# One weight row moved to GpSimd's queue, and sixteen matmuls moved ahead of a projection, in a fused state-space and feed-forward block

## The chip, the core and the metric

The kernel runs on one core of a Trainium2 chip. The metric is the device time of one execution in microseconds (us). A core has five instruction streams that run side by side and wait for each other through semaphores: TensorE (PE, with its weight loads shown apart as PEld), VectorE (DVE), ScalarE (ACT), GpSimd (POOL) and SyncE (SP), which here only issues DMAs. SP, ACT and POOL issue DMAs; sixteen DMA engines carry them out.

## The reference

The input x has 2048 tokens of 512 numbers. The result is the sum of x and two branches, both fed by the layer norm of x:

```
xn  = layernorm(x)                              # mean and variance over the 512 features
A   = 2 Re(C h) + xn * Dskip,  h_t = Lam_bar h_(t-1) + B_bar xn_t     # complex, 512 states
B   = (silu(xn w_gate) * (xn w_up)) w_down      # 512 -> 1376 -> 512
out = x + A + B
```

Lam_bar and B_bar come from the parameter vectors Lambda_re, Lambda_im and log_dt. All tensors are bf16.

## The kernel before

**Tiling.** Tokens go in 16 tiles of 128 and in four chunks (0 to 3) of four tiles. Matmuls contract over 128 rows and give 128x512 results in PSUM, which has eight banks of that size; `bank()` hands them out in turn. The 1376 hidden features are ten full blocks of 128 and a rest of 96 (`FR`). `xnT` holds the normalized tokens transposed, which is what the matmuls need.

**Stages on PE.** (1) Warm-up matmuls (line 703). (2) The head: chunk 0 has no transposed tokens yet, so tiles 0 and 1 are transposed by matmuls against an identity (`raw_mm`, line 237), the mean is taken off by matmuls (`cT_mean`, line 245), and ACT and DVE copy the results out (`raw_copy`, line 252). Then `row_mm(which, k)` (line 747) multiplies both tiles with row k of the up weights (which = 0) or of the gate weights (which = 1): four matmuls of 128x512 for each k, four rows each, all at line 506. A row here is 128 of the 512 input features by the first 1024 hidden ones, 256 KB. (3) A transposition of the parameter vectors (`prm_transpose`, line 278), tile 2's transposition, and the other products of chunk 0 (lines 506 and 805). (4) Chunk 0's projection on the 512 states (`bproj_tile`, line 387, 32 matmuls with the transposed B matrix `BT`). (5) `gateup_last(0)` (line 548; matmuls at line 555): the last 96 features of chunk 0, 16 matmuls of 128x192, four evacuations on ACT (lines 560 and 561), and a product on DVE with a transposing DMA behind it (line 571). (6) The same for the other chunks: projections, gate and up (line 462), output matmuls with `w_down` (lines 620 and 630) and with C (line 643).

**Order.** Each engine's order is that of the program text (`manual_schedule`). DVE's long operations (tables, scans, rotations) stand in a backlog; `pump(us)` takes operations from it as PE time passes, `need(tag)` drains it up to a tag, and `multiply(keep)` runs waiting products from the list `products`.

**Loads at the start.** SP issues, in this order: tile 0 of x (line 128), the four up rows (lines 132 and 122), gate rows 0 and 1, tile 2 of x, gate row 2, tile 3, gate row 3, the last feature group of both weights (`load_w1`, line 118, tile `w_end`), and x of chunk 1 (line 146). ACT issues tile 1 of x (line 130). POOL builds the identity (`make_identity`, called at line 126), clears `prm_rows` (line 143), loads the three parameter vectors into it (line 145, three DMAs of 1 KB) and then computes the powers for the layer norm (line 199). The semaphores of SP's and ACT's DMAs are used in turn by eights: an issue waits until the DMA eight places before it has landed.

**Further DMAs.** Line 258 transposes chunk 0 into `xnT` in two parts, line 150 loads `BT` in two transposing DMAs (real and imaginary part), line 262 transposes chunks 1 to 3. At line 896, SP copies x of chunks 0 to 2 to the output in eight pieces of 192 rows, onto which POOL later adds results (lines 604 and 653).

Of the kernel before, what the change touches and what calls it, by code (L numbers as in the profile page):

```python
# [23 lines left out]
def kernel(  # L24
# [17 lines left out]
    nc = tc.nc  # L42
# [4 lines left out]
    CW = 512  # L47
    HW = CW // 2
    NT = L // 128
    NCH = L // CW  # L50
    TPC = CW // 128
    KD = D // 128
# [25 lines left out]
    def bank(shape=(128, CW), dtype=F32):  # L78
        return psum.tile(list(shape), dtype, name="ps")

    def flat(ap3):
        return ap3.rearrange("p q j -> p (q j)")
# [4 lines left out]
    wu_v = B_w_up.rearrange("(k p) f -> p k f", p=128)  # L87
# [8 lines left out]
    wu01 = const.tile([128, KD, FE], BF16, name="wu01")  # L96
# [24 lines left out]
    def load_row(q, t, view, k):  # L121
        q.dma_start(out=t[:, k, :], in_=view[:, k, 0:FE])  # L122

    HK = KD // 2
    ident = const.tile([128, 128], BF16, name="ident")
    make_identity(nc, ident[:])
    minus_mean = const.tile([128, 128], BF16, name="minus_mean")
    nc.sync.dma_start(out=xall[:, 0, :], in_=x_v[:, 0, :])  # L128
    nc.vector.memset(xall[:, 1, 0:2], 0.0)
    nc.scalar.dma_start(out=xall[:, 1, :], in_=x_v[:, 1, :])  # L130
    nc.scalar.preload_act_table_set("silu_and_others")
    for k in range(KD):
        load_row(nc.sync, wu01, wu_v, k)
    for k in range(HK):
        load_row(nc.sync, wg01, wg_v, k)
# [69 lines left out]
    def norm_dve(n):  # L205
        c, i = divmod(n, TPC)
        nc.vector.tensor_scalar(out=xn_tile(c)[:, :, i, :], in0=by_k(xall[:, n, :]), scalar1=mv[:, n, 0:1],
                                scalar2=rstd[:, n:n + 1], op0=ALU.subtract, op1=ALU.mult)
# [9 lines left out]
    SW = TPC - 1  # L218
# [57 lines left out]
    def prm_transpose():  # L276
        pp = bank()[:, 0:128]
        nc.tensor.matmul(pp, lhsT=prm_rows[:], rhs=ident[:], start=True, stop=True)  # L278
        return pp
# [4 lines left out]
    def exp_pool(out, in_):  # L284
        nc.gpsimd.tensor_tensor(out=out, in0=e_t[:], in1=in_, op=ALU.pow)
# [96 lines left out]
    def bproj_tile(c, part, q):  # L382
        if c not in u_tiles:
            u_tiles[c] = ssm.tile([128, 2, NQ, CW], BF16, name="u16", bufs=2)
        ps = bank()
        for k in range(KD):
            nc.tensor.matmul(ps[:] if c else by_k(ps[:]), lhsT=BT[:, part, k, q * 128:(q + 1) * 128],  # L387
                             rhs=xnT[:, c, k, :] if c else xnT0[:, k], start=(k == 0), stop=(k == KD - 1))
        nc.scalar.copy(out=u_tiles[c][:, part, q, :], in_=ps[:])  # L389
# [67 lines left out]
    products = []  # L457
# [10 lines left out]
    def gu_tile(c):  # L468
        if c not in gu_tiles:
            gu_tiles[c] = gut.tile([128, FT, CW], BF16, name="guT")  # L470
        return gu_tiles[c]
# [8 lines left out]
    def gu_rest(c):  # L480
        return gu_more_rest[:] if c == 2 else gu_tile(c)[:, FT - 1, 0:RT * 128]
# [21 lines left out]
    def sw_mm(ps, groups, gi, i, k0=0, k1=KD):  # L503
        a, b = fgroups[gi]
        for k in range(k0, k1):
            nc.tensor.matmul(ps[:, 0:(b - a) * 128], lhsT=tokens(i, k), rhs=groups[gi][:, k, 0:(b - a) * 128],  # L506
                             start=(k == 0), stop=(k == KD - 1))
# [35 lines left out]
    def g0_dma(a, b):  # L543
        nc.sync.dma_start_transpose(out=runs(gu_tiles[0][:, a:b, :]), in_=g0[:, a:b].rearrange("p f i d -> p (f i d)"))
# [3 lines left out]
    def gateup_last(c):  # L548
        gl = g_last[c % 2][:] if c else g0[:, FT - 1, 0:RT]
        u = up_p.tile([128, RT, 128], BF16, name="ul", bufs=2)  # L550
        for h in range(0, TPC, 2):
            ps = bank()[:, 0:4 * FR].rearrange("p (i w f) -> p i w f", i=2, w=2)
            for i in range(2):
                for k in range(KD):
                    nc.tensor.matmul(ps[:, i],  # L555
                                     lhsT=xnT[:, c, k, (h + i) * 128:(h + i + 1) * 128] if c else xnT0[:, k, h + i, :],
                                     rhs=w_end[:, k, :, FL - FE:FL - FE + FR], start=(k == 0), stop=(k == KD - 1))
            two = slice(h * RB, (h + 2) * RB)
            src = ps.rearrange("p i w (j f) -> p w j i f", f=RB)
            nc.scalar.activation(out=gl[:, :, two].rearrange("p j (i f) -> p j i f", f=RB), in_=src[:, 0], func=ACT.Silu)  # L560
            nc.scalar.copy(out=u[:, :, two].rearrange("p j (i f) -> p j i f", f=RB), in_=src[:, 1])

        def product():
            V.tensor_tensor(out=gl, in0=gl, in1=u[:], op=ALU.mult)
            if c:
                nc.sync.dma_start_transpose(out=gu_rest(c).rearrange("p (n t) -> p n t", t=128),
                                            in_=gl.rearrange("p i d -> p (i d)"))
            else:
                a = fgroups[1][1]
                n = (FT - 1 - a) * TPC + RT  # L570
                nc.sync.dma_start_transpose(
                    out=flat(gu_tile(0)[:, a:FT, :])[:, 0:n * 128].rearrange("p (n t) -> p n t", t=128),
                    in_=g0[:, a:FT].rearrange("p f i d -> p (f i d)")[:, 0:n * 128])
        products.append(product)
# [93 lines left out]
    def step():  # L668
        for item in backlog[0:AHEAD + 1]:
            if item[2] is not None:  # L670
                item[2]()
                item[2] = None
        cost, op, _, _ = backlog.pop(0)
        op()
        owed[0] -= cost

    def pump(us):

        owed[0] += us
        while backlog and owed[0] >= backlog[0][0] * 0.5:  # L680
            step()
        if not backlog:
            owed[0] = 0.0

    def multiply(keep):

        while len(products) > keep:
            products.pop(0)()
            owed[0] -= 0.65

    def need(tag):

        while any(item[3] == tag for item in backlog):
            step()


    GU = 8 * 0.2163
# [49 lines left out]
    def row_mm(which, k):  # L747
        for i in range(2):
            for gi in range(2):
                sw_mm(pair[which][i][gi], (U, G)[which], gi, i, k, k + 1)  # L750
# [8 lines left out]
            sw_up(gi, i, pair[0][i][gi])  # L759
    for n in range(2):  # L760
        norm_dve(n)
    row_mm(1, 0)
    pp = prm_transpose()
    ln_stats(2)
    center(2)
# [2 lines left out]
    ln_rstd(3, 4)  # L768
    prm_copy(pp)
    exp_pool(dt_t[:], ldt)  # L770
    for k in range(1, SW):
        row_mm(1, k)
    t2 = bank()
    for k in range(KD):
# [46 lines left out]
    def bproj_chunk(c):  # L821
        need(f"ln{c}")
        for part in range(2):
            for q in range(NQ):
                bproj_tile(c, part, q)
                pump(BP)
                multiply(0 if q else 1)
# [32 lines left out]
    def queue_ssm(c):  # L860
        fwd, back = ssm_ops(c)
        queue(f"ssm{c}", fwd + back)

    need("ln0")
    for part in range(2):
        for q in range(NQ):
            bproj_tile(0, part, q)
            pump(BP)
            multiply(0 if q else 1)
# [5 lines left out]
    queue("cf", c_ops())  # L875
    need("ln1")
    g0_dma(0, fgroups[1][1])
    gateup_last(0)
    pump(GU / 2)
    bproj_chunk(1)  # L880
    load_down()
    for part, src in enumerate((A_C_re, A_C_im)):
# [8 lines left out]
    gateup_chunk(1)  # L891
    nc.gpsimd.dma_start(out=dsk_bc[:], in_=A_Dskip.partition_broadcast(128))
    bproj_chunk(2)
    piece = (NCH - 1) * CW // 8
    for a in range(0, (NCH - 1) * CW, piece):
        nc.sync.dma_start(out=out[0, a:a + piece, :], in_=A_x[0, a:a + piece, :])
    queue_ssm(2)
    gateup_chunk(2)
    out_chunk(0)
# [45 lines left out]
```

## Time and profile before

| | us |
|---|---|
| median of three runs | 177.66 (177.65 to 178.03) |
| the profiled execution, whole | 178.12 |
| its span in the trace | 176.0 |
| PE busy | 171.0 |
| DVE busy | 157.4 |
| ACT busy | 102.3 |
| POOL busy | 27.1 |

The span runs from the first to the last instruction of the trace; 2.12 us of the execution lie around it. In the rows of the trace the first number is the start in us from the span's start, the second the duration in us (for merged rows, of the whole group); what follows is engine, line, operation, result, operands and count. "SPq" and "ACTq" are issues of DMAs from SP's and ACT's queues. "Busy" of a matmul counts from its start to its modelled end, and neighbouring matmuls overlap: four of them in a row start 0.22 us apart.

### The profile page before, as it was taken

The numbers are of one execution on the slowest core, as the hardware profiler recorded it, in microseconds if no ns is written. First come the engines' busy times: TensorE is split into PE (matmuls) and PEld (weight loads), VectorE is DVE, ScalarE is ACT, GpSimd is POOL, SyncE is SP. The second block draws the span as 40 slices with busy tenths as digits, with TensorE's granted clock in tenths as the row PEclk, the third lists the DMA queues.
The fourth block names the chain that finished last, engine by engine and source line by source line (L and its number), as shares of the span: only waits on it lengthen the run. The fifth ranks groups of instructions, "written<-read, shape, count | busy, mean of one in ns | idle before, by whom it ended". The sixth has DMA issues, their size and how long they took to land.

```text
span 176.0 us, 2435 instructions
## 1 busy us (share of the span) xinstructions
PE 171.0 (97%) x878; PEld 82.0 (47%) x894; DVE 157.4 (89%) x260; ACT 102.3 (58%) x188; POOL 27.1 (15%) x36
## 2 busy tenths in 40 slices
PE   8899999999999999999999999999999999999993
PEld 5444445564444464444444444446444444444542
DVE  3767999999999999999999999999999999589642
ACT  3179589794996689976044362014666652983100
POOL 5234110022000000000302500014100000530700
PEclk9999999999999999999999999999999999999999
DMA  5998969999999300220005830006310000597741
GB/s 152 370 342 80 194 110 181 303 202 293 169 207 274 115 4 0 50 61 0 2 4 111 94 34 0 0 4 68 53 22 0 0 4 0 70 164 124 93 89 60
DMA packets 34027, 18.05 MB, mean 103 GB/s; under 512 B 24512, under 2 KB 32832, under 8 KB 33888
## 3 DMA queue, kind: packets, MB, share of 16 engines
q1 hardware_dynamic: 30272, 14.39, 35.0%
q0 software_dynamic: 3456, 3.28, 14.6%
q10 hardware_dynamic: 288, 0.23, 0.4%
q8 instruction: 7, 0.11, 0.3%
q14 instruction: 4, 0.03, 0.1%
HBM read 8.33 MB, written 5.24 MB: 77 GB/s over the span
## 4 chain that ended last, share of the span: by engine, by line
PE 94%; DMA 3%; issue 1%; SPq 0%; ACT 0%; DVE 0%; ACTq 0%
PE ps L462 29%; PE ps L630 20%; PE ps L643 16%; PE ps L387 16%; PE ps L506 7%; PE ps L555 3%; DMA wu<-in_B_w_up_dram 3%; PE ps L805 2%; PE ps L620 2%; ACT u L489 0%; SPq L122 0%; SPq L128 0%; DVE xall L646 0%; PE ps L237 0%; PE ps L278 0%
## 5 line engine op out<-in xcount | busy, mean ns | idle before, releaser
L429 DVE TENSOR_TENSOR_SCAN g<-r_t,car,u 128x512 bf16<-128x512 f32 x24 | 28.8, 1263 | 0.0
L643 PE MATMUL ps<-CF,wt 128*128 128x512 bf16 (+2 forms) x133 | 28.2, 366 | 0.2
L387 PE MATMUL ps<-xnT,BT 128*128 128x512 bf16 x125 | 28.1, 379 | 0.2
L630 PE MATMUL ps<-wd_sb,guT 128*128 128x512 bf16 (+2 forms) x129 | 26.5, 362 | 0.1
L462 PE MATMUL ps<-xnT,wu 128*128 128x512 bf16 x94 | 24.5, 379 | 0.2
L462 PE MATMUL ps<-xnT,wg 128*128 128x512 bf16 x93 | 24.3, 379 | 0.1
L389 ACT CAST u<-ps 128x512 bf16<-128x512 f32 x32 | 17.8, 591 | 5.0 <-PE ps L387 4.1
L489 ACT CAST u<-ps 128x512 bf16<-128x512 f32 x30 | 17.8, 592 | 4.8 <-PE ps L462 4.8
L643 PEld LDWEIGHTS <-wt 128*128 128x128 bf16 x136 | 12.9, 98 | 15.0 <-DVE xall L600 0.4
L387 PEld LDWEIGHTS <-BT 128*128 128x128 bf16 x128 | 12.5, 98 | 14.9 <-DMA BT<-in_A_B_re_dram 0.3
L630 PEld LDWEIGHTS <-guT 128*128 128x128 bf16 x130 | 12.4, 98 | 13.8
L199 POOL TENSOR_TENSOR rstd<-ve,neg_half 128x1 f32<-128x1 f32 (+1 forms) x7 | 7.0, 1001 | 73.0 <-DVE ve L198 72.6
L652 ACT CAST res<-ps 128x512 bf16<-128x512 f32 x12 | 6.9, 582 | 18.5 <-PE ps L643 18.5
L592 ACT ACTIVATE xr<-xall,nb,rstd 128x512 bf16<-128x512 bf16 x16 | 11.8, 804 | 8.7 <-DVE xall L600 5.0
L653 POOL DMA_DIRECT2D out_dram<-res x12 | 10.5, 1043 | 35.6 <-ACT res L652 30.0
L462 PEld LDWEIGHTS <-wu 128*128 128x128 bf16 x96 | 9.4, 98 | 11.3
L488 ACT ACTIVATE guT<-ps 128x512 bf16<-128x512 f32 x20 | 12.1, 604 | 4.0 <-PE ps L462 3.6
L462 PEld LDWEIGHTS <-wg 128*128 128x128 bf16 x96 | 9.3, 98 | 10.6
L212 ACT ACTIVATE xn<-xall,nb,rstd 128x512 bf16<-128x512 bf16 x8 | 6.3, 816 | 8.8 <-DVE nb L202 8.8
L189 DVE BATCH_NORM_STATS2 stats<-xall 128x6 f32<-128x512 bf16 x16 | 10.8, 675 | 0.6 <-DMA xall<-in_A_x_dram 0.6
L462 PE MATMUL ps<-xnT,w_end 128*128 128x512 bf16 x47 | 10.8, 379 | 0.1
L397 DVE TENSOR_TENSOR pm<-g,c 128x2048 bf16<-128x2048 bf16 x8 | 9.8, 1222 | 0.1
(132 smaller groups left out, 235.3 us busy)
## 6 DMA issues: line engine op xcount, KB each, us to landing
out_dram<-in_A_x_dram SPq DMA_DIRECT2D x8, 192.0 KB, 3.2
out_dram<-res POOLq DMA_DIRECT2D x12, 128.0 KB, 3.1
out_dram<-xall POOLq DMA_DIRECT2D x3, 512.0 KB, 6.4
wd_sb<-in_B_w_down_dram SPq DMA_DIRECT2D x1, 1280.0 KB, 7.8
wu<-in_B_w_up_dram SPq DMA_DIRECT2D x4, 256.0 KB, 4.9
wg<-in_B_w_gate_dram SPq DMA_DIRECT2D x4, 256.0 KB, 5.5
xall<-in_A_x_dram SPq DMA_DIRECT2D x1, 1024.0 KB, 7.0
xall<-in_A_x_dram SPq DMA_DIRECT2D x1, 512.0 KB, 6.1
```

Of the source, the lines that this page charges most:

```text
L189: nc.vector.bn_stats(out=stats[:, n, 0, :], in_=xall[:, n, :])
L387: nc.tensor.matmul(ps[:] if c else by_k(ps[:]), lhsT=BT[:, part, k, q * 128:(q + 1) * 128], rhs=xnT[:, c, k, :] if c else xnT0[:, k], star ...
L389: nc.scalar.copy(out=u_tiles[c][:, part, q, :], in_=ps[:])
L429: V.tensor_tensor_scan(out=g()[:, part, q, :], data0=r_t[:, q:q + 1].to_broadcast([128, CW]), data1=u_tiles[c][:, part, q, :], initial=ini ...
L462: nc.tensor.matmul(ps[:fs, lo:hi], lhsT=wslice(groups, fi, k), rhs=xnT[:, c, k, lo:hi], start=(k == 0), stop=(k == KD - 1))
L488: nc.scalar.activation(out=gu(c, fi, fi + 1)[:fs, 0, :], in_=psg[:fs], func=ACT.Silu)
L489: nc.scalar.copy(out=u_pair[c][:fs, fi % 2, :], in_=psu[:fs])
L506: nc.tensor.matmul(ps[:, 0:(b - a) * 128], lhsT=tokens(i, k), rhs=groups[gi][:, k, 0:(b - a) * 128], start=(k == 0), stop=(k == KD - 1))
L592: nc.scalar.activation(out=box["xr"][:], in_=xall[:, n, :], func=ACT.Identity, scale=rstd[:, n:n + 1], bias=nb[:, n:n + 1])
L630: nc.tensor.matmul(o_tiles[n, b][:, 0:hi - lo], lhsT=gu(c, fi, fi + 1)[:, 0, i * 128:(i + 1) * 128], rhs=wd_sb[:, fi, lo:hi], start=(fi == ...
L643: nc.tensor.matmul(o[:, 0:hi - lo], lhsT=w_tiles[c][:, part, q, i * 128:(i + 1) * 128], rhs=CF[:, part, q, lo:hi], start=False, stop=(part ...
L653: nc.gpsimd.dma_start(out=out_v[:, n, lo:hi], in_=res[:, lo:hi], accum_op=ALU.add)
```

## The change

Five edits:

1. Up row 1 is issued by POOL as its first work after the start, ahead of `make_identity`. On SP its place falls away, and every load behind it moves up by one.
2. The identity, the clearing of `prm_rows` and the three loads of parameter vectors stand behind that DMA on POOL.
3. `prm_transpose()` on PE moves from behind gate row 0 to behind gate row 1.
4. `gateup_last(0)` moves ahead of chunk 0's projection, with its `pump`. Its product is taken out of the list and put back at the old place; the order of DVE's instructions is the same. On ACT the four evacuations move ahead of the projection's casts, and the first sine of a table comes behind two casts in place of three.
5. The copies of x to the output are nine, the first two of 96 rows.

```
@@ -123,13 +123,14 @@
     ident = const.tile([128, 128], BF16, name="ident")
+    load_row(nc.gpsimd, wu01, wu_v, 1)
     make_identity(nc, ident[:])
     minus_mean = const.tile([128, 128], BF16, name="minus_mean")
     nc.sync.dma_start(out=xall[:, 0, :], in_=x_v[:, 0, :])
     nc.vector.memset(xall[:, 1, 0:2], 0.0)
     nc.scalar.dma_start(out=xall[:, 1, :], in_=x_v[:, 1, :])
     nc.scalar.preload_act_table_set("silu_and_others")
-    for k in range(KD):
+    for k in (0, *range(HK, KD)):
         load_row(nc.sync, wu01, wu_v, k)
@@ -759,7 +760,8 @@
-    row_mm(1, 0)
+    for k in range(HK):
+        row_mm(1, k)
     pp = prm_transpose()
@@ -768,7 +770,7 @@
     exp_pool(dt_t[:], ldt)
-    for k in range(1, SW):
+    for k in range(HK, SW):
         row_mm(1, k)
@@ -862,6 +864,9 @@
     need("ln0")
+    gateup_last(0)
+    pump(GU / 2)
+    last0 = products.pop()
     for part in range(2):
         for q in range(NQ):
             bproj_tile(0, part, q)
@@ -875,8 +880,7 @@
     need("ln1")
     g0_dma(0, fgroups[1][1])
-    gateup_last(0)
-    pump(GU / 2)
+    products.append(last0)
     bproj_chunk(1)
@@ -891,9 +895,10 @@
-    piece = (NCH - 1) * CW // 8
-    for a in range(0, (NCH - 1) * CW, piece):
-        nc.sync.dma_start(out=out[0, a:a + piece, :], in_=A_x[0, a:a + piece, :])
+    piece = (NCH - 1) * CW // 16
+    cuts = [0, piece, *range(2 * piece, (NCH - 1) * CW + 1, 2 * piece)]
+    for a, b in zip(cuts, cuts[1:]):
+        nc.sync.dma_start(out=out[0, a:b, :], in_=A_x[0, a:b, :])
```

`HK` is 2, `KD` 4 and `SW` 3.

More of the change, by code (lines that the diff above doesn't have):

```diff
@@ L125 @@
     ident = const.tile([128, 128], BF16, name="ident")
+    load_row(nc.gpsimd, wu01, wu_v, 1)
     make_identity(nc, ident[:])
@@ L131 @@
     nc.scalar.preload_act_table_set("silu_and_others")
-    for k in range(KD):
+    for k in (0, *range(HK, KD)):
         load_row(nc.sync, wu01, wu_v, k)
@@ L761 @@
         norm_dve(n)
-    row_mm(1, 0)
+    for k in range(HK):
+        row_mm(1, k)
     pp = prm_transpose()
@@ L770 @@
     exp_pool(dt_t[:], ldt)
-    for k in range(1, SW):
+    for k in range(HK, SW):
         row_mm(1, k)
@@ L864 @@
     need("ln0")
+    gateup_last(0)
+    pump(GU / 2)
+    last0 = products.pop()
     for part in range(2):
@@ L877 @@
     g0_dma(0, fgroups[1][1])
-    gateup_last(0)
-    pump(GU / 2)
+    products.append(last0)
     bproj_chunk(1)
@@ L893 @@
     bproj_chunk(2)
-    piece = (NCH - 1) * CW // 8
-    for a in range(0, (NCH - 1) * CW, piece):
-        nc.sync.dma_start(out=out[0, a:a + piece, :], in_=A_x[0, a:a + piece, :])
+    piece = (NCH - 1) * CW // 16
+    cuts = [0, piece, *range(2 * piece, (NCH - 1) * CW + 1, 2 * piece)]
+    for a, b in zip(cuts, cuts[1:]):
+        nc.sync.dma_start(out=out[0, a:b, :], in_=A_x[0, a:b, :])
     queue_ssm(2)
```

## The prediction

> **What bounds the kernel now.** I read the head of the page, then the chain that ended last, then PE's waits.
>
> ```profile
> PE 171.0 (97%) x878; PEld 82.0 (47%) x894; DVE 157.4 (89%) x260; ACT 102.3 (58%) x188; POOL 27.1 (15%) x36
> ```
> ```profile
> 1.65 4.80 DMA wu<-in_B_w_up_dram
> ...
> 6.49 3.61 PE ps L506 x16
> ...
> 172.82 0.46 PE ps L643 x8
> ```
> ```profile
> PE ps L506 <- DMA wu<-in_B_w_up_dram: 0.6, 1, 0.6
> ```
>
> PE is the bound. From 6.49 us to the end the chain is PE, matmul behind matmul, and beside its start PE has one wait in the whole span: for a row of up weights. What reaches the time is therefore when PE's gapless run begins and whether something new breaks it. The timeline of the head shows the wait at its place, and SP's issues show when loads landed, since the later ones wait for the one eight places ahead:
>
> ```profile
> 0.74 0.40 SPq L128 DMA_DIRECT2D xall<-in_A_x_dram  x1
> 1.20 1.83 SPq L122 DMA_DIRECT2D wu<-in_B_w_up_dram  x4
> 4.82 1.07 PE L506 MATMUL ps<-wu,CF 128*128 128x512 bf16 x4
> 6.47 0.33 SPq L122 DMA_DIRECT2D wg<-in_B_w_gate_dram  x1
> 6.49 2.75 PE L506 MATMUL ps<-wu,CF 128*128 128x512 bf16 x12 [0.60 <-DMA wu<-in_B_w_up_dram]
> 7.12 0.39 SPq L118 DMA_DIRECT2D w_end<-in_B_w_gate_dram  x1
> 7.80 0.37 SPq L118 DMA_DIRECT2D w_end<-in_B_w_up_dram  x1
> 8.61 0.37 SPq L146 DMA_DIRECT2D xall<-in_A_x_dram  x1
> 9.94 0.22 PE L278 MATMUL ps<-ident,prm_rows 128*128 128x128 bf16 x1
> ```
> ```profile
> DMA to landing us min/median/max: 2.9/4.9/5.2
> ```
>
> The last row is the four up rows. Row 0 landed at 1.20 + 2.9 = 4.1, row 1 at 1.65 + 4.80 = 6.45, row 2 about 7.1, row 3 about 7.8, gate row 0 about 8.6 (the issues at 7.12, 7.80 and 8.61). PE multiplied row 0 from 4.82 and then stood until row 1 was there.
>
> The pitch of these matmuls is (2.75 - 0.38) / 11 = 0.216 us (a matmul by itself is 0.38), a row of four 0.86. So the twelve from 6.49 would join gaplessly to a row that began at 6.49 - 0.86 = **5.63**. Call that start s; before, s is 5.63. The row-0 matmuls took 1.07 in place of 3 x 0.216 + 0.38 = 1.03, so without the wait s would be 4.82 + 0.04 = **4.86**. The most that can be won is 5.63 - 4.86 = 0.77 us. With a start s, row 1 is due at s + 0.86, row 2 at s + 1.73, row 3 at s + 2.59, gate row 0 at s + 3.45, gate row 1 at s + 4.31.
>
> **The change part by part.**
>
> *Up row 1 on POOL.* POOL's first work stands at 0.74 now; the DMA takes that place. What its issue costs and when 256 KB from POOL land, this trace doesn't show; the nearest rows do:
>
> ```profile
> 0.74 0.20 POOL masks.py:197 MEMSET ident<- 128x128 bf16 x1 [0.29 <-POOLq L929]
> 1.78 0.70 POOL L145 DMA_DIRECT2D prm_rows<-in_A_Lambda_re_dram  x1 [0.31 <-POOL prm_rows L143]
> 95.35 0.95 POOL L653 DMA_DIRECT2D out_dram<-res  x1 [8.42 <-ACT res L652]
> ```
> ```profile
> out_dram<-res POOLq DMA_DIRECT2D x12, 128.0 KB, 3.1
> out_dram<-xall POOLq DMA_DIRECT2D x3, 512.0 KB, 6.4
> xall<-in_A_x_dram ACTq DMA_DIRECT2D x1, 128.0 KB, 2.5
> dsk_bc<-in_A_Dskip_dram POOLq DMA_DIRECT2D x1, 128.0 KB, 8.0
> prm_rows<-in_A_log_dt_dram POOLq DMA_DIRECT2D x1, 1.0 KB, 5.4
> ```
>
> Issue: 0.70 (four pieces) to 0.95 (128 pieces, as here); I take 0.9. Landing: between 3.1 (128 KB) and 8.0 (beside transposes, which the head has none of). On the line from 3.1 at 128 KB to 6.4 at 512 KB, 256 KB take 4.2, so row 1 lands at 0.74 + 4.2 = 4.9; the ends are 3.8 and 8.7. It is due at 4.86 + 0.86 = 5.72, so the value that I take has 0.8 in hand.
>
> *The rows behind it on SP* move up one place: row 2 has row 1's place and row 3 row 2's. If a place lands when it did, row 2 is there at 6.45 (due 6.59), row 3 at 7.1 (due 7.45), gate row 0 at 7.8 (due 8.31) and gate row 1 at 8.6 (due 9.17): nothing waits. That needs room on the DMA engines for POOL's 256 KB beside them. The windows of the head:
>
> ```profile
> 2.75:3.50 0.75, 0.75 (x9) 0.50 (x6) 0.43 (x3) 0.00 (x0) 0.75 (x2) 1.00 1.09 374
> 3.50:4.25 0.75, 0.75 (x9) 0.69 (x8) 0.67 (x4) 0.27 (x1) 0.04 (x1) 1.00 0.76 139
> 5.75:8.75 3.00, 2.40 (x12) 1.07 (x11) 2.41 (x8) 0.05 (x1) 1.24 (x2) 1.00 1.05 388
> ```
>
> The last column is GB/s. From 3.50 to 4.25 the rate falls from 374 to 139, which leaves 0.75 us x 235 = 176 KB unmoved: two thirds of a row. A row that is already queued from POOL can fill it; I take that as the likelier reading. What is won at the outside is the 0.77.
>
> What sharing costs: 256 KB at 374 to 388 GB/s are 0.7 us. If all of row 1 ran ahead of row 0, row 0 would land at 4.1 + 0.7 = 4.8, just in time for 4.82. Tile 1 of x has less room: it lands at about 0.90 + 2.5 = 3.4 (ACT issues it at 0.90) and is used at once:
>
> ```profile
> 0.90 0.37 ACTq L130 DMA_DIRECT2D xall<-in_A_x_dram  x1
> 1.34 0.20 DVE L729 TENSOR_SCALAR minus_mean<-ident 128x128 bf16<-128x128 bf16 x1 [0.41 <-POOL ident masks.py:199]
> 3.07 0.42 DVE L229 SCALAR_TENSOR_TENSOR xnT<-xall 128x256 bf16<-128x256 bf16 x1 [1.53 <-DMA xall<-in_A_x_dram]
> 3.48 0.43 DVE L229 SCALAR_TENSOR_TENSOR xnT<-xall 128x256 bf16<-128x256 bf16 x1
> ```
>
> Between no delay and half of row 1 in front of it (0.35) I take 0.15 on s.
>
> *Identity and parameter vectors behind it.* DVE took the identity up at 1.34 for 0.20; 0.9 later that ends at 2.44. PE's first use of either follows the landing of tile 0, on which DVE waits until 3.07. Nothing, with 0.6 in hand. The last vector was issued at 3.02 and landed 5.4 later, at 8.4; now about 9.3. PE transposed at 9.94; behind gate row 1 and with s 0.62 earlier it comes at 9.94 + 0.86 - 0.62 = 10.2. Nothing, with 0.9 in hand; were the cover gone, each us of lateness would cost PE one.
>
> *gateup_last(0) ahead of the projection.* The amount of PE work is unchanged. What it does is a cover for `BT`:
>
> ```profile
> 15.77 4.41 SPq L150 DMA_TRANSPOSE BT<-in_A_B_re_dram  x1
> 22.31 1.03 PE L805 MATMUL ps<-w_end,xnT 128*128 128x512 bf16 x4
> 23.10 6.65 PEld L387 LDWEIGHTS <-BT 128*128 128x128 bf16 x32 [0.26 <-DMA BT<-in_A_B_re_dram]
> 30.08 1.48 PE L555 MATMUL ps<-w_end,xnT 128*128 128x192 bf16 x16
> 30.94 0.33 ACT L560 ACTIVATE guT<-ps 128x192 bf16<-128x192 f32 x1
> ```
>
> The weight load waited for `BT` until 23.10, and PE came to it at 22.31 + 0.86 = 23.17: no time in hand. SP's issue at 15.77 hangs on DVE and on other transposes, not on PE, so a PE that is 0.62 earlier would stand about 0.55 here. The sixteen matmuls take 1.48 - 0.16 = 1.32 and cover it. Their operands `w_end` and `xnT` are there: line 805 has just used both kinds, and the second part of `xnT` is issued before `BT`. The four evacuations (0.33 each, 1.3) delay ACT's casts; PE has eight banks to run ahead by, 0.86 us each in this stage. Nothing; without that cover up to 1.3.
>
> *Behind that* PE meets data earlier that DVE and DMA still bring at the old time. The closest meeting that I find is chunk 1's projection:
>
> ```profile
> 25.09 1.79 SPq L262 DMA_TRANSPOSE xnT<-xn  x1
> 31.40 7.07 PE L387 MATMUL ps<-xnT,BT 128*128 128x512 bf16 x31
> ```
> ```profile
> xnT<-xn SPq DMA_TRANSPOSE x3, 4.3
> ```
>
> 25.09 + 4.3 = 29.4, due at 31.40 - 0.62 = 30.8, 1.4 in hand. Nothing gives it back.
>
> *Nine copies in place of eight* add one issue on SP (5.49 for eight, 0.69 each) at 51.66; SP's next issue there stands at 71.71, waiting for DVE. Nothing.
>
> ```profile
> 51.66 5.49 SPq L896 DMA_DIRECT2D out_dram<-in_A_x_dram  x8
> 71.71 1.19 SPq L566 DMA_TRANSPOSE gu_more_rest<-g_last  x1
> ```
>
> **The sum.** 0.77 won, 0.15 lost on tile 1 of x: 0.62 us. A profiled execution of 178.12 becomes 177.50. The median of the runs, 177.66, lies 0.46 under the profiled one; the same 0.62 off gives **177.04**. A difference of 0.2% is 0.36 us, about what a measurement of this kernel can tell from no change.
>
> **The rivals.**
>
> *The bytes only change places* (gain 0.26, 177.40). If the engines had no room, the rows up to row 2 together would land when they did, the last of them, now row 2, at 7.1. Then s = 7.1 - 1.73 = 5.37, and 5.63 - 5.37 = 0.26. For it: 374 and 388 GB/s in the windows on both sides. Against it: the 139 between them. [...]
>
> *The stall moves onto row 0* (slower by 0.57, 178.23). The fall to 139 begins 1.7 us after POOL's first DMA issue at 1.78. Row 0 had just landed, and row 1 came 2.35 after it (6.45 - 4.1), though a row takes 0.7. If POOL's first DMA brings that stall, the stall comes about a us earlier, upon tile 1 and row 0, with row 1's bytes between row 0's. Row 0 would land between 4.1 + 0.7 + 0.75 = 5.55 and row 1's old 6.45. From 5.63 on the change loses. I take 6.2: s = 6.2, 0.57 late. For it: the coincidence, and row 0's having been safe before. Against it: the later row 2 to gate row 0 came 0.65 to 0.8 apart while POOL's vectors were still under way. [...]
>
> *The vectors come too late* (gain 0.2, 177.46). A load of 1 KB that took 5.4 us stands now behind 256 KB in POOL's queue. If it lands at 10.6 in place of 9.3, PE stands for 0.4 at the transposition. Decides from 10.2.
>
> **How the numbers follow.** Forecast 0.52, bytes changing places 0.18, stall on row 0 0.24, late vectors 0.06. The forecast runs from the full 0.77 (176.89) to 177.3, where tile 1 costs 0.5. Faster by over 0.2%: the forecast and a little of the second, 0.54; within 0.2%: the rest of the two small gains, 0.22; slower by over 0.2%: 0.24. The range goes from 176.85 to 178.2, and so leaves out half of the stall's cases and the far tail of POOL's landing.
>
> **What would show it.** Right: PE's wait for `wu` is gone, the row-0 matmuls start by about 5.0 and all up rows follow at 0.86; the projection's first weight load doesn't wait for `BT`; PE's other rows stand about 0.6 earlier to the end. The first rival: a wait of about 0.5 for row 2. The second: row-0 matmuls that start after 5.6, with a low rate in the windows before 3.5. The third: a wait at the transposition, line 279 now. Wrong altogether, if PE's run is later broken by a wait that the list above doesn't have.

## The result and the profile after

The changed kernel takes 178.41 us (median of 22 runs, 177.37 to 180.71), the kernel before in the same session 177.75 us (22 runs, 177.10 to 178.43). The ratio is 1.0032 with a 95% interval of [1.0018, 1.0046]: slower by 0.32%, where 0.35% faster was forecast. The time lies above the predicted range, too. A few runs over 1.5% above the fastest of their kernel, such as the one of 180.71, are left out of all ratios and of the medians of the experiments below. The profiled execution of the changed kernel took 178.41 us with a span of 176.4, against 178.12 and 176.0. All of its line numbers are one to five higher than those of before.

The head of the page and PE's waits in the profile after, the same lines that opened the prediction:

```profile
PE 171.3 (97%) x878; PEld 82.1 (47%) x894; DVE 157.4 (89%) x260; ACT 102.7 (58%) x188; POOL 27.7 (16%) x37
```
```profile
PE ps L507 <- DMA wu<-in_B_w_up_dram: 0.8, 1, 0.8
```

The wait for up weights was to vanish. It went from 0.6 to 0.8 us. The chain that ended last (start, duration, what) names the DMA:

```profile
1.29 5.61 DMA wu<-in_B_w_up_dram
6.94 4.48 PE ps L507 x20
...
173.76 0.29 DVE xall L647
```

The DMA that starts at 1.29 is GpSimd's row 1; it lands at 1.29 + 5.61 = 6.90, where SP's row 1 had landed at 6.45. The last operation on DVE in the chain starts at 173.76. In the chain of before the same operation stands here:

```profile
173.31 0.29 DVE xall L646
```

So the end is 0.45 later. The timeline of the head in the profile after shows that this is all made at its start:

```profile
1.20 1.36 SPq L122 DMA_DIRECT2D wu<-in_B_w_up_dram  x3
1.29 0.73 POOL L122 DMA_DIRECT2D wu<-in_B_w_up_dram  x1 [0.84 <-POOLq L934]
2.01 0.23 POOL masks.py:197 MEMSET ident<- 128x128 bf16 x1
4.68 1.48 PE L507 MATMUL ps<-wu,CF 128*128 128x512 bf16 x4
6.94 2.75 PE L507 MATMUL ps<-wu,CF 128*128 128x512 bf16 x12 [0.78 <-DMA wu<-in_B_w_up_dram]
7.26 0.39 SPq L118 DMA_DIRECT2D w_end<-in_B_w_gate_dram  x1
7.92 0.38 SPq L118 DMA_DIRECT2D w_end<-in_B_w_up_dram  x1
8.63 0.37 SPq L147 DMA_DIRECT2D xall<-in_A_x_dram  x1
9.53 1.89 PE L507 MATMUL ps<-wg,CF 128*128 128x512 bf16 x8
11.26 0.22 PE L279 MATMUL ps<-ident,prm_rows 128*128 128x128 bf16 x1
```

Gate row 0 starts at 9.53. In the profile before it stands here:

```profile
9.08 1.03 PE L506 MATMUL ps<-wg,CF 128*128 128x512 bf16 x4
```

It is 0.45 late, and 173.76 - 9.53 = 164.23 is what 173.31 - 9.08 was. Behind gate row 0 nothing has changed. The same holds for the profiles of all kernels below: from gate row 0 to the last operation on DVE it is 164.23 us in each but the first (164.55). What they win or lose is made ahead of gate row 0, or behind the last operation, and nothing gives it back in between. The outside of the span is a little shorter (2.0 in place of 2.1), so the profiled times differ by 0.29.

Three readings of this timeline go against the forecast. GpSimd starts its DMA at 1.29, though its memset stood at 0.74 before. The three SP issues at 7.26, 7.92 and 8.63 tell that the DMAs eight places ahead have landed: these are now row 2, row 3 and gate row 0. Before, the issues at 7.12, 7.80 and 8.61 told the same of the same three rows. So a row that moved up a place on SP landed when it had landed before, not when its place had. And the four matmuls of row 0 took 1.48 in place of 1.07, with nothing to wait for in between. That last row turned out to be the one to follow.

The windows of the head after (the last column is GB/s):

```profile
2.75:3.50 0.75, 0.75 (x10) 0.66 (x8) 0.67 (x4) 0.00 (x0) 0.44 (x2) 1.00 1.05 333
3.50:4.25 0.75, 0.75 (x10) 0.75 (x9) 0.56 (x3) 0.27 (x1) 0.75 (x3) 1.00 0.68 183
5.75:8.75 3.00, 2.22 (x11) 0.96 (x10) 2.40 (x8) 0.00 (x0) 1.25 (x2) 1.00 1.05 372
```

The fall between 3.50 and 4.25 is still there: 183 GB/s against 139, which is 0.75 us x 44 = 33 KB more, not the 176 KB that GpSimd's row was to fill.

### The profile page after: what moved, and what is told of

Read it like the earlier page. It is cut to its first block, busy times and chain, and to the rows that moved or that the text cites. A ratio compares the mean times of both kernels' runs of the same rounds, so it can differ in the third digit from the quotient of the medians.

```text
span 176.4 us, 2437 instructions
## 1 busy us (share of the span) xinstructions
PE 171.3 (97%) x878; PEld 82.1 (47%) x894; DVE 157.4 (89%) x260; ACT 102.7 (58%) x188; POOL 27.7 (16%) x37
## 4 chain that ended last, share of the span: by engine, by line
PE 94%; DMA 3%; issue 1%; ACT 0%; DVE 0%; ACTq 0%; POOLq 0%
PE ps L463 29%; PE ps L631 20%; PE ps L644 16%; PE ps L388 16%; PE ps L507 7%; DMA wu<-in_B_w_up_dram 3%; PE ps L556 3%; PE ps L807 2%; PE ps L621 2%; ACT u L490 0%; DVE xall L647 0%; PE ps L238 0%; PE ps L279 0%; ACTq L490 0%; POOLq L934 0%
```

## The experiments

Two theories stood at the start. One: GpSimd's row is late and is the whole loss. The rival: other parts of the change (the moved matmuls, the ninth copy) cost it. The first eight kernels part these; the last six ask why the row costs, and why nothing is won even without its wait. Ratios are to the kernel before, run on the same chip, with 95% intervals.

### Row 1 by GpSimd alone

Before, with edits 1 and 2 only:

```
+    load_row(nc.gpsimd, wu01, wu_v, 1)
     make_identity(nc, ident[:])
-    for k in range(KD):
+    for k in (0, *range(HK, KD)):
         load_row(nc.sync, wu01, wu_v, k)
```

> The kernel before with up row 1 issued by GpSimd ahead of the identity, and nothing else of the change. Theory (the row's own way through GpSimd's queue is the whole loss): row 1 lands near 6.9 us in place of 6.45, PE's wait for it stays (0.6 to 0.9), and the time is 0.2 to 0.7 us over the kernel before. Rival (the loss comes from the reordered vectors, the moved 16 matmuls or the nine copies): within 0.2 us of the kernel before.

Measured: 178.42, ratio 1.0039 [1.0020, 1.0059]. This part alone is as slow as the whole change. The timeline of its profile:

```profile
1.29 0.72 POOL L122 DMA_DIRECT2D wu<-in_B_w_up_dram  x1 [0.84 <-POOLq L930]
5.83 2.96 PE L507 MATMUL ps<-wu,CF 128*128 128x512 bf16 x12 [0.28 <-DMA wu<-in_B_w_up_dram]
8.62 1.03 PE L507 MATMUL ps<-wg,CF 128*128 128x512 bf16 x4
9.75 0.22 PE L279 MATMUL ps<-ident,prm_rows 128*128 128x128 bf16 x1
```

Again GpSimd starts at 1.29. In this one execution its row was there at 5.8, over a us earlier than in the profile after (6.90): the landing differs that much between these two executions. The chain shows a second wait, for a row of SP:

```profile
1.65 5.21 DMA wu<-in_B_w_up_dram
6.90 2.75 PE ps L507 x12
```

The DMA that starts at 1.65 is SP's second, row 2. It lands at 6.86, where PE was due at 5.83 + 0.86 = 6.69, so with GpSimd's row early PE stands 0.21 for row 2. All in all gate row 0 is at 8.62, 0.46 earlier than before: this execution (178.05) is the second fastest of the twelve, and its profile doesn't show what the others lost. The transposition of the vectors, due at 8.62 + 0.86 = 9.48, came at 9.75. So without edit 3 PE stands 0.27 for the vectors.

### Everything but the row

After, with row 1 back on SP:

```
-    load_row(nc.gpsimd, wu01, wu_v, 1)
     make_identity(nc, ident[:])
-    for k in (0, *range(HK, KD)):
+    for k in range(KD):
```

> The changed kernel with up row 1 back on SP, second of the up rows; the three other edits stay. Theory: within 0.2 us of the kernel before, row 1 lands at 6.4 to 6.5, PE waits 0.6 for it. Rival (these edits make the loss): 0.3 to 0.7 us slower.

Measured: 178.39, ratio 1.0027 [1.0012, 1.0043]. That was a surprise: the rest alone costs nearly as much, although its gate row 0 starts at 8.63, 0.45 before that of the kernel before. In its profile PE has no wait for up weights at all, although all four rows come by SP as before:

```profile
4.90 3.90 PE L506 MATMUL ps<-wu,CF 128*128 128x512 bf16 x16
```

Its span runs on for 3.1 us behind the last DVE start, where before has 2.7. The next two kernels take the rest apart.

### The ninth copy alone, and the rest without it

First, before with nine copies (edit 5 alone). Second, before with edits 3 and 4 alone.

```
-    piece = (NCH - 1) * CW // 8
-    for a in range(0, (NCH - 1) * CW, piece):
-        nc.sync.dma_start(out=out[0, a:a + piece, :], in_=A_x[0, a:a + piece, :])
+    piece = (NCH - 1) * CW // 16
+    cuts = [0, piece, *range(2 * piece, (NCH - 1) * CW + 1, 2 * piece)]
+    for a, b in zip(cuts, cuts[1:]):
+        nc.sync.dma_start(out=out[0, a:b, :], in_=A_x[0, a:b, :])
```

> The kernel before with nine copies of x to the output in place of eight, and nothing else. Theory (the ninth DMA shifts which of the eight semaphores the last store uses, and the waits that end the program then follow it one by one): last landing to the end of the span 1.35 us in place of 0.9, time 0.3 to 0.6 us over the kernel before. Rival (a copy more in the middle of the span costs nothing, and what was seen with the row back on SP is due to the moved matmuls): within 0.2 us of the kernel before.

> The changed kernel with up row 1 back on SP and eight copies: only the moved transposition of the vectors and the moved 16 matmuls remain. Theory: 0.3 to 0.6 us under the same with nine copies, level with the kernel before or up to 0.2 us under it. Rival (the moved matmuls cost ACT or PE time): 0.3 us or more over the kernel before.

Measured: the ninth copy alone 178.40, ratio 1.0027 [1.0013, 1.0041]; edits 3 and 4 alone 177.80, ratio 0.9997 [0.9982, 1.0011]. So the moved matmuls and the moved transposition are level, and a copy that nothing waits for costs 0.27%. SP's waits at the end, of before and then of the kernel with the ninth copy (engine, what for, us in total):

```profile
SPq L940 <- DMA out_dram<-xall: 0.5, 1, 0.5
```
```profile
SPq L941 <- DMA out_dram<-xall: 1.0, 1, 1.0
```

SP's last waits stand at the program's end, and with the ninth copy the one for the store is 0.5 us longer. SP and ACT use their semaphores in turn by eights (before, gate row 3 is issued at 6.47, 0.02 behind the landing of row 1, eight DMAs ahead of it), so with one DMA more in that count the last store falls on another semaphore. The numbers of all kernels fit: from the last DVE start to the end of the span it is 2.7 us where the count is that of before or one lower, and 3.12 to 3.15 in the three kernels where it is one higher (everything but the row, the ninth copy alone, and row 1 by ACT with nine copies, next). That the place in the turn is the reason is argued from this count; that the ninth copy costs this is shown. In the change itself the count is that of before, since a row has left SP: there the ninth copy is free, and it is not the loss.

### Row 1 by ScalarE

After, with row 1 issued by ACT instead (nine copies), and the same with eight:

```
-    load_row(nc.gpsimd, wu01, wu_v, 1)
...
+    load_row(nc.scalar, wu01, wu_v, 1)
     nc.scalar.preload_act_table_set("silu_and_others")
```

> The changed kernel with up row 1 issued by ACT behind tile 1 of x, in place of GpSimd. Theory (GpSimd's queue delivers it slowly, 3.25 to 6.75 us in the trace): from ACT it lands by 5.0 to 6.4, PE's wait shrinks to 0 to 0.5 or passes to row 2, and the time is 0.1 to 0.6 us under the kernel before. Rival (any second queue beside SP's only takes turns with row 0 on engines that are full): row 1 lands at 6.4 to 7.0, row 0 later than 4.1, and the time is level or up to 0.6 us over.

> The changed kernel with up row 1 on ACT's queue behind tile 1 of x, and eight copies, so that the count of SP's and ACT's DMAs is that of the kernel before. Theory (GpSimd's queue is what is late; a row from ACT is not, and the tail is back): 0.0 to 0.6 us under the kernel before. Rival (any second queue takes from row 0 and tile 1 what it gives to row 1): level with the kernel before or over it by up to 0.3 us.

Measured: with nine copies 178.39, ratio 1.0022 [1.0005, 1.0039], no more than what the ninth copy costs by itself; with eight 177.66, ratio 0.9987 [0.9970, 1.0004]. With nine copies the profile has a wait for SP's row 2:

```profile
6.53 1.89 PE L507 MATMUL ps<-wu,CF 128*128 128x512 bf16 x8 [0.23 <-DMA wu<-in_B_w_up_dram]
```

With eight the profile is what the prediction wanted of the change: no wait for up weights, and sixteen row matmuls in one gapless run. Yet at most 0.3% comes of it in the timed runs, and no difference at all is within the interval.

### The identity first

After, with `make_identity` ahead of GpSimd's row:

```
-    load_row(nc.gpsimd, wu01, wu_v, 1)
     make_identity(nc, ident[:])
+    load_row(nc.gpsimd, wu01, wu_v, 1)
```

> The changed kernel with the identity built first on GpSimd and row 1 issued behind it. Theory (landing follows the issue, since the queue delivers at a fixed pace): issue 0.2 to 0.6 us later than at 1.29, landing near 7.2, time 0.2 to 0.4 us over the changed kernel. Rival (the landing is set by what SP's queue leaves free): landing stays at 6.9, time level with the changed kernel.

Measured: 178.54, ratio 1.0034 [1.0017, 1.0052]. The chain and the timeline of its profile:

```profile
1.48 6.06 DMA wu<-in_B_w_up_dram
```
```profile
7.58 2.75 PE L507 MATMUL ps<-wu,CF 128*128 128x512 bf16 x12 [1.34 <-DMA wu<-in_B_w_up_dram]
```

The DMA starts only 0.19 later than in the change (1.48 against 1.29), and so being first buys little. The wait grew to 1.34 us. The time ratio is not told apart from that of the change, so the size of this one wait belongs to its execution.

### No loads of GpSimd at all

Before, without the three parameter vectors; `prm_rows` is set to -0.5 instead, so the decays and steps are those of constant parameters.

```
-    nc.gpsimd.memset(prm_rows[:], 0.0)
+    nc.gpsimd.memset(prm_rows[:], -0.5)
-    for i, v in enumerate((A_Lambda_re, A_Lambda_im, A_log_dt)):
-        nc.gpsimd.dma_start(out=prm_rows[i * NQ:(i + 1) * NQ, :], in_=v.rearrange("(q j) -> q j", j=128))
```

> The kernel before without the three loads of parameter vectors on GpSimd; the rows they would fill are set to -0.5, so this leaves the loads of Lambda and log_dt out. It tells whether GpSimd's DMAs cause the fall of the DMA rate between 3.5 and 4.25 us. Theory (they do: GpSimd's first DMA stalls the engines): rate there over 300 GB/s, PE's wait for row 1 gone or under 0.2, time 0.2 to 0.6 us under the kernel before. Rival (the fall comes with the weight rows themselves): rate there 139 to 290 as in the runs so far, time within 0.2 us of the kernel before.

Measured: 177.94, ratio 1.0005 [0.9989, 1.0021]. Its window of the head:

```profile
3.50:4.25 0.75, 0.75 (x10) 0.64 (x8) 0.68 (x5) 0.27 (x1) 0.00 (x0) 1.00 0.64 180
```

With no DMA of GpSimd in the head the rate still falls to 180 GB/s. So the fall needs no DMA of GpSimd, as the second rival had it. Its cause stays open.

### Row 3 by GpSimd, and two rows by ScalarE

After, with row 3 on GpSimd in place of row 1; and the version with ACT and eight copies, with rows 1 and 3 on ACT.

```
-    load_row(nc.gpsimd, wu01, wu_v, 1)
+    load_row(nc.gpsimd, wu01, wu_v, KD - 1)
-    for k in (0, *range(HK, KD)):
+    for k in range(KD - 1):
         load_row(nc.sync, wu01, wu_v, k)
...
     load_row(nc.scalar, wu01, wu_v, 1)
+    load_row(nc.scalar, wu01, wu_v, KD - 1)
-    for k in (0, *range(HK, KD)):
+    for k in (0, HK):
         load_row(nc.sync, wu01, wu_v, k)
```

> The changed kernel with up row 3, the last that PE needs, on GpSimd's queue in place of row 1; rows 0 to 2 go by SP in order. Theory (the row that goes by GpSimd is late by its own way, and lands between 5.6 and 7.3 us): row 3 is due only at about 7.5, so the loss goes; level with the kernel before to 0.4 us under it. Rival (GpSimd's 256 KB slow all other rows of the head by sharing the engines): row 1 by SP lands later than 6.5, and the time stays 0.3 to 0.7 us over the kernel before.

> Up rows 1 and 3 on ACT's queue behind tile 1 of x, rows 0 and 2 on SP, eight copies, the moved matmuls kept. Theory (a second hardware queue fills the fall of the rate after 3.5 us): all up rows in time, 0.3 to 0.8 us under the kernel before. Rival (more rows on ACT only take turns with row 0 and tile 1): level with row 1 alone on ACT, 0 to 0.4 us under the kernel before, or over it.

Measured: row 3 by GpSimd 178.47, ratio 1.0036 [1.0016, 1.0056]; two rows by ACT 178.61, ratio 1.0039 [1.0023, 1.0055]. PE's row matmuls in the two timelines:

```profile
6.55 2.75 PE L507 MATMUL ps<-wu,CF 128*128 128x512 bf16 x12 [0.71 <-DMA wu<-in_B_w_up_dram]
```
```profile
7.55 1.89 PE L508 MATMUL ps<-wu,CF 128*128 128x512 bf16 x8 [0.44 <-DMA wu<-in_B_w_up_dram]
```

With two rows on ACT it is SP's row 2 that comes late, at 7.5: the bytes change places. With row 3 on GpSimd the profile shows the old wait for SP's row 1, at 6.55 against 6.49 before, while the timed runs are as slow as the change. GpSimd's own row isn't late here. The profile's time from its issue to its landing is the last number of this line:

```profile
wu<-in_B_w_up_dram POOLq DMA_DIRECT2D x1, 256.0 KB, 4.9
```

It starts at 1.28 and so lands at 6.2; PE comes to it at 6.55 + 1.73 = 8.28. So the theory that the lateness of GpSimd's own row is the whole loss does not hold here, and the time is the one that its rival forecast, by which GpSimd's bytes hold up the rows of SP. The profiled execution (178.18) is among the faster ones, so this profile does not show what the others lost, and the rival isn't shown by it either.

### Row 1 by ScalarE alone, and the ACT version again

Before, with row 1 on ACT as the only edit; and the version with ACT and eight copies once more, unchanged.

```
+    load_row(nc.scalar, wu01, wu_v, 1)
     nc.scalar.preload_act_table_set("silu_and_others")
-    for k in range(KD):
+    for k in (0, *range(HK, KD)):
         load_row(nc.sync, wu01, wu_v, k)
```

> The kernel before with up row 1 on ACT's queue and nothing else: vectors transposed behind gate row 0, the 16 matmuls at their old place. Theory (the moved 16 matmuls are a cover for BT that an earlier head needs): PE's first weight load of chunk 0's projection waits for BT 0.2 to 0.8, and the time is 0.1 to 0.5 us over the next run's. Rival (BT moves with the head): no such wait, level with the next run.

> The same kernel as the run with row 1 on ACT and eight copies, to narrow its interval: theory 0.1 to 0.4 us under the kernel before in both together; rival: level with it.

Measured: 177.68, ratio 1.0001 [0.9984, 1.0018], and 177.81, ratio 0.9995 [0.9979, 1.0012]. Neither beats before. The two executions of the same kernel, the ACT version with eight copies, are the most telling pair of the study. The first took 176.89 us, the second 178.03. Their timelines of PE:

```profile
3.20 0.61 PE L238 MATMUL ps<-ident,xall 128*128 128x128 bf16 x4
...
3.85 0.43 PE L238 MATMUL ps<-ident,xall 128*128 128x128 bf16 x4
...
4.45 3.62 PE L507 MATMUL ps<-wu,CF 128*128 128x512 bf16 x16
7.90 1.89 PE L507 MATMUL ps<-wg,CF 128*128 128x512 bf16 x8
```
```profile
3.22 0.61 PE L238 MATMUL ps<-ident,xall 128*128 128x128 bf16 x4
...
3.88 0.63 PE L238 MATMUL ps<-ident,xall 128*128 128x128 bf16 x4
...
4.95 4.20 PE L507 MATMUL ps<-wu,CF 128*128 128x512 bf16 x16
8.98 1.89 PE L507 MATMUL ps<-wg,CF 128*128 128x512 bf16 x8
```

Tile 0 is taken up at the same time (3.20 and 3.22), PE waits for no weights in either, and gate row 0 differs by 1.08 us, nearly all of the 1.14 between the times. The difference is in PE itself. Sixteen matmuls took 3.62 = 15 x 0.216 + 0.38 in the first, 0.58 more in the second, and the four small transpositions at 3.85 and 3.88 took 0.43 and 0.63. PE runs slowly at first and turns to full speed (a pitch of 0.216) at a moment that differs between executions.

### Row 1 not awaited, with GpSimd's transfer and without

After, and before, each with row 0's weights in the place of row 1's for tiles 0 and 1. Row 1 of the up weights is thus left out of these two tiles; its transfer takes place as before, and PE waits for it only later.

```
+                if which == 0 and k == 1:
+                    a, b = fgroups[gi]
+                    nc.tensor.matmul(pair[0][i][gi][:, 0:(b - a) * 128], lhsT=tokens(i, 1),
+                                     rhs=U[gi][:, 0, 0:(b - a) * 128], start=False, stop=False)
+                    continue
                 sw_mm(pair[which][i][gi], (U, G)[which], gi, i, k, k + 1)
```

> The kernel after, but in the head the matmuls of up row 1 for tiles 0 and 1 take row 0's weights, so that PE waits for GpSimd's row only much later; up row 1 is left out of these two tiles. The transfer is there and only its lateness is harmless. Theory 'the row's own lateness is the whole loss': rows 2 and 3 come on SP where rows 1 and 2 came before (6.45 and 7.1), just ahead of their due times, PE has no wait for wu above 0.1 us, gate row 0 starts at about 8.3 and the time is 0.4 to 0.8 us under before (ratio 0.9955 to 0.998). Theory 'GpSimd's bytes hold up the rows of SP': a wait for row 2 stays (0.3 us or more), gate row 0 starts at 8.8 or later, and the ratio is 0.9985 or more.

> The kernel before with the same replacement, up row 1 by SP: what not awaiting row 1 gives by itself. Row 2 landed at about 7.1 and is due at 4.86 + 1.73 = 6.59, so by both theories a wait for wu of about 0.3 to 0.5 us is left, gate row 0 starts at about 8.8, and the ratio is 0.9985 (0.997 to 1). If the time falls by more than 0.3%, the rows' landing has more room than the one profile shows, and the first kernel of this pair has to be read against this one.

Measured: after without the wait 177.85, ratio 1.0000 [0.9984, 1.0017]; before without the wait 177.80, ratio 0.9995 [0.9980, 1.0010]. With GpSimd's transfer in place, but not awaited, the 0.32% is gone. So in the change the loss comes about by PE's wait for this row. Why the row is late, by its own way or because it shares the engines with SP's rows, this pair doesn't tell. And neither theory's profile came: for the first kernel one forecast a gain of 0.4 us or more, the other a wait for row 2, and for the second both forecast that wait. There is no wait in either profile, and no gain; the times are those that the second theory gave (ratios of 0.9985 or more). PE's rows in the two timelines:

```profile
4.93 1.82 PE L507 MATMUL ps<-wu,CF 128*128 128x512 bf16 x4
6.59 1.03 PE L753 MATMUL ps<-wu,CF 128*128 128x512 bf16 x4
7.45 1.89 PE L507 MATMUL ps<-wu,CF 128*128 128x512 bf16 x8
```
```profile
4.85 1.71 PE L506 MATMUL ps<-wu,CF 128*128 128x512 bf16 x4
6.40 1.03 PE L752 MATMUL ps<-wu,CF 128*128 128x512 bf16 x4
7.26 1.89 PE L506 MATMUL ps<-wu,CF 128*128 128x512 bf16 x8
```

The first kernel's timeline also has SP's issue that tells of row 2:

```profile
7.31 0.39 SPq L118 DMA_DIRECT2D w_end<-in_B_w_gate_dram  x1
```

Row 2 landed at about 7.3 and PE came to it at 7.45: just in time, because PE was late itself. Row 0 takes 1.82 and 1.71 us, the next row 1.03. Cut to a narrow window, the timeline gives the pitch of two neighbours: of the second kernel at 5.28, and of the ACT version's first execution at 5.53.

```profile
5.28 1.06 PE L506 MATMUL ps<-wu,CF 128*128 128x512 bf16 x2
```
```profile
5.53 0.59 PE L507 MATMUL ps<-wu,CF 128*128 128x512 bf16 x2
```

Two slow matmuls take 1.06, one by itself 0.63, so they start 0.43 apart; two at full speed take 0.59, one 0.38, and start 0.21 apart. That is half speed against full. A matmul at half speed costs 0.21 us, four of them 0.86: as much as a whole row. The granted clock in the profile's windows reads 1.00 all through the head, so it doesn't show this; the pitch does. The turn falls into the transpositions at 3.85 in the ACT version's first execution, into row 0 in the profiles of before and after (1.07 and 1.48 for four), and to the end of row 0, between 6.1 and 6.6, in the last pair. Earliest of all sixteen profiles it falls at about 3.7, with row 1 on ACT and nine copies; in nine of the sixteen it comes later than in the profile of before. PE's first matmul starts at 0.78 in each, and the turns lie between 2.9 and 5.9 us behind it. What sets the moment, the traces don't show.

## Why the prediction was wrong

Two steps failed above all. Row 1 was to be there at 4.9, with 0.8 in hand, and landed at 6.90 in the profile after; PE stood for it until 6.94, and this landing alone sets the 0.45 that the profile loses. And the 0.77 on offer rested on a start of 4.86, which PE didn't keep where it turned to full speed late; so even a row in time need not gain it.

**The start without the wait (4.86) failed.** I took 1.07 us for four row-0 matmuls as nearly the gapless 1.03, and so 0.216 as PE's pitch wherever nothing is waited for. That holds only behind the turn to full speed (0.43 us apart ahead of it). In the profile of before the turn happened to fall at the start of row 0; where it falls later, PE is busy with slow matmuls during what looks like the wait for row 1. Removing the wait then uncovers PE's own slowness, as the last pair shows: row 1 isn't awaited, and gate row 0 stands at 9.0 and 9.2. So the 0.77 us aren't on offer in every execution; with everything but the row, and so with all rows on SP, the profile had no wait to remove. Four measurements without GpSimd fit this: row 1 by ACT with no wait in the profile gives 0.9987, 0.9995 and (alone) 1.0001, and row 1 not awaited at all gives 0.9995. The best of these is 0.13%, and all four intervals hold no change. That this turn is the reason in the timed runs too is argued: a profile shows one execution of each kernel. In executions with an early turn a wait for row 2 may take its place, as in the first kernel (0.21) and with row 1 by ACT and nine copies (0.23).

**GpSimd's start (0.74) failed too.** As GpSimd's first work a DMA begins at 1.28 or 1.29 in the four profiles that have it, 0.55 behind the place of the memset. I put the DMA in the memset's slot without a row of a first DMA.

**The landing (4.2 after the start, ends 3.1 to 8.0) was mis-sized.** It took 5.61 in the profile after, 6.06 with the identity first, 4.5 in the row alone and 4.9 with row 3 on GpSimd. The line through two sizes came from later stages; where the first of the 128 KB stores stands (95 to 99 us) the engines move 146 GB/s, in the head 372. With the late start even the shortest of these is behind the due time: 1.29 + 4.5 = 5.79 against 5.72. In the profile after row 1 was there at 6.90, where PE was done with row 0 at 4.68 + 1.48 = 6.16. That the wait (0.78) is as long as the time that was to be in hand is chance.

**"A place lands when it did" failed.** Row 2 was there at 7.26, not 6.45 (and at 7.3 with row 1 not awaited). SP's issue behind row 2 comes at 6.88 to 7.86 in the four profiles with row 1 on GpSimd and at 6.26 to 7.35 in the six with all up rows on SP: though one row less is ahead of it, row 2 is rather later. Had GpSimd's row come in time and PE turned to full speed early, PE would have stood for row 2: s = 7.26 - 1.73 = 5.53, a gain of 0.10 in place of 0.77. The premise of the first rival, that the bytes only change places, came nearest for GpSimd's row, and its wait for row 2 is there where GpSimd's row came early (0.21, in the row alone). Its gain of 0.26 didn't come, because it took row 1 to be in time: with s = 5.37 that asks for 5.37 + 0.86 = 6.23, and GpSimd's row came at 6.90.

**The fall of the rate** was not filled (33 of 176 KB), and it is there without a DMA of GpSimd too. With row 1 on ACT the window of 3.50 to 4.25 carries 355 to 396 GB/s in four profiles, so room was there for ACT's row; but with SP alone it ranges from 139 to 314 too, and the time gained nothing.

**The second rival** had the sign, and nearly the size: 0.57 late was its price, 0.45 in the profile, 0.66 between the medians, 0.57 by the ratio (0.32% of 177.75). Its mechanism was wrong, and the size is luck: the stall stays on row 1, and row 0 starts at 4.68, a little earlier than before. So the 0.15 for tile 1 of x cost nothing in this profile either. (The range's inner bound was a slip: with 0.5 for tile 1 the sum gives 177.39, not 177.3.)

**Edits costed at nothing.** The identity: right, DVE takes it up at 2.64 and PE isn't late. The vectors: right, and edit 3 is needed, since the row alone stands 0.27 for them. `gateup_last` ahead of the projection: right as to cost. In the timeline after, the projection joins it gaplessly (23.62 + 1.32 = 24.94):

```profile
23.62 1.48 PE L556 MATMUL ps<-w_end,xnT 128*128 128x192 bf16 x16
...
24.94 7.29 PE L388 MATMUL ps<-xnT,BT 128*128 128x512 bf16 x33
```

Its use as a cover for `BT` couldn't show where PE came later; where PE came 0.29 earlier without it (row 1 by ACT alone), PE had no wait for `BT` either. There `BT` was issued earlier than before, at 15.25 in place of 15.77, so its issue does move with the head:

```profile
15.25 3.13 SPq L151 DMA_TRANSPOSE BT<-in_A_B_re_dram  x1
```

Nine copies: nothing, but not for the reason that I gave. By itself the ninth costs 0.27%; in the change it takes the place of the row that left SP's count.

**What stays open.** In the change, the loss is PE's wait for GpSimd's row: the row alone is as slow, the rest is level, and with the row not awaited the loss is gone. How much of the 5.6 us to land is GpSimd's issue path and how much the company of SP's rows isn't settled. The run with row 3 on GpSimd lost as much with that row in time, which speaks for the company; its profile doesn't show where: in it SP's rows 1 and 2 are awaited beside GpSimd's transfer, which the pair with row 1 not awaited doesn't test. The profiles of ACT's single row put gate row 0 at 8.48 on average (four, 7.90 to 8.98), those with SP alone at 8.96 (five, 8.63 to 9.32); the timed runs show less than half of that, and the moment of PE's turn to full speed, which no run here sets, is the likely reason, not a shown one.

## What to carry to other kernels

Before a wait near a kernel's start is priced, look at the pitch of the matmuls ahead of it: while PE runs at half speed (here 0.43 us apart in place of 0.216), the wait covers slow work that comes to light once the wait is gone. A time to land is to be taken from a stage with the same traffic, and from more than one execution; a first DMA's start from a first DMA, not from another operation's place. Where the end of a kernel is one store, compare the stretch behind the last operation too: a DMA added elsewhere lengthened it here by 0.4 to 0.5 us.

## What the runs showed of the hardware

- PE's first matmuls run at half speed (0.43 us apart for 128x512 in place of 0.216) until a moment that lay between about 3.7 and 6.7 us of the span in sixteen profiles. Two executions of one kernel had gate row 0 1.08 us apart through it.
- A DMA that GpSimd issues first begins at 1.29, while a memset at the same place began at 0.74; behind the identity it begins at 1.48. Its 256 KB then took 4.5 to 6.1 us to land beside SP's rows.
- Row 1 by SP, issued at the same place, had landed by 5.5 in one profile and not before 6.7 in another. So a difference of half a us between two single profiles of the head can be scatter.
- One DMA more on SP or ACT lengthened the stretch behind the last operation by 0.4 to 0.5 us in three kernels of three; SP's wait for the last store grew from 0.5 to 1.0.
